# Taking the residual of a token mixer from crossbar DMA transposes, added by VectorE at the output evacuation, instead of from identity matmuls

## The chip, the cores and the metric

The kernel runs on one core of one Trainium2 chip. The metric is the device time of one execution in microseconds (us). The profile comes from one execution each; its span is some 1.8 us shorter than the time of the same run. PE is TensorE, PEld its weight loads, DVE is VectorE, ACT is ScalarE, POOL is GpSimd, SP is SyncE (SPq its DMA queue). An evacuation is the instruction that takes a finished result out of PSUM, and the head is the time before the first evacuation of an output, some 75 to 80 us.

## The reference, cut to what matters

Eight batches of 448 tokens, 12 heads of 64. Attention with squared ReLU gives x; then a mixer works along tokens and along channels:

```python
x = attention(q, k, v)                       # (8, 448, 768)
h = relu(x.transpose(0, 2, 1) @ w_tok1) @ w_tok2
u = x + h.transpose(0, 2, 1)                 # mixed tokens
out = u + relu(u @ w_ch1) @ w_ch2            # the outer "u +" is the residual of this change
```

## The kernel before

The mixed tokens are held channel-major: `uT_sb` has channels on the partitions, as the first channel layer needs them. The output is token-major. So the residual has to be transposed, which the kernel does inside the output's accumulation: three identity matmuls per unit of 128 tokens x 384 channels.

```python
def token2(s):                               # s = batch * 6 + head pair
    ...                                      # two matmuls into ps
    nc.vector.tensor_tensor(out=uT_tiles[b // 2][:, p, off : off + S],
                            in0=ps[:, :S], in1=xT[b % 2][:, p, :S], op=ALU.add)

def channel2(bb, t, half):                   # 56 of these
    ...
    for e in range(EC):                      # 12 matmuls, 384 columns each
        nc.tensor.matmul(ps[:, :HN], lhsT=r2[:, e, tok], rhs=wc2[:, e, cols], ...)
        if e == 0:
            for g in range(CC // 2):         # 3 identity matmuls: the residual
                nc.tensor.matmul(ps[:, g * 128 : (g + 1) * 128],
                                 lhsT=uT[:, half * (CC // 2) + g, tok], rhs=ident, ...)
    nc.vector.tensor_copy(o[:, cols], ps[:, :HN])
    ...                                      # store by SyncE when half == 1
```

The channel units (`channel1`, `channel2`) of a batch are queued when its last head pair is mixed, and fill the gaps of the attention of later batches. Inputs are loaded by GpSimd three pairs ahead. The channel weights are loaded by GpSimd too, between the inputs, in the first 60 us (`wc1` in two pieces, `wc2` in four).

## Time and profile before

| | before |
|---|---|
| time, median (range) | 428.83 us (427.82 to 429.5, 4 runs) |
| span of the profiled run (its time: 429.84 us, above the four runs) | 428.0 us |
| identity matmuls | 168 |
| SyncE's DMA queue | 4,480 packets, 8.7% of 16 engines' span |

The profile lists instructions in groups. In the view by line with shapes kept apart, a line reads: source line, engine, operation, tiles and shapes, count; busy us and mean ns of one; idle us of the engine before it and what ended that. The two groups that the change replaces, in the kernel before:

```profile
L356 DVE COPY out_sb<-m_ps 128x384 f32<-128x384 f32 x56 | 31.2, 558 | 90.1 <-PE m_ps L338 90.1
...
L348 PE MATMUL m_ps<-ident,uT_sb 128*128 128x128 bf16 x168 | 18.5, 219 | 0.0
```

The 219 ns are the record of one matmul from start to modelled end, and neighbouring records overlap. Here are stretches in the kernel before (start and end, length, busy us of PE, PEld, DVE, ACT, POOL, granted TensorE clock with 1.00 for full, DMA share, GB/s):

```profile
20.00:40.00 20.00, 15.80 (x168) 7.39 (x162) 17.40 (x36) 14.45 (x20) 14.95 (x23) 1.00 1.27 165
60.00:80.00 20.00, 19.64 (x158) 10.20 (x157) 9.39 (x19) 11.75 (x18) 7.87 (x12) 1.00 0.90 123
```

From 20 us on the DMA engines are more than full (over 1, because records of queues overlap), and it takes until about 68 us until the weights are in (the last load is issued at 59.5 us and lands 8.2 us later).

### The profile page before, as it was taken

The page shows a single profiled execution, that of the slowest core. Times are in us where ns is not written, and L with a number is a line of the kernel's source. Part 1 is how long each engine was busy: PE and PEld are TensorE (multiplying, and loading weights), DVE is VectorE, ACT ScalarE, POOL GpSimd, SP SyncE. Part 2 cuts the span into 40 slices and gives each one's busy share as a digit, 9 for nine tenths or more (in the row PEclk, how much of TensorE's full clock was granted, in tenths as well). Part 3 has the DMA queues.
Part 4 walks back from the last instruction along what each step waited for, and adds up shares of the span by engine and source line. Part 5 has one row for each costly group of instructions (what it writes and reads, how often), then busy time and mean ns, then how long its engine had stood idle before and what let it go on. Part 6 is the DMA issues. An engine that isn't in the chain of part 4 may idle for free.

```text
span 428.0 us, 8076 instructions
## 1 busy us (share of the span) xinstructions
PE 410.1 (96%) x3345; PEld 218.7 (51%) x3345; DVE 230.0 (54%) x450; ACT 212.7 (50%) x313; POOL 130.8 (31%) x196
## 2 busy tenths in 40 slices
PE   6878999999999999999999999999999999999995
PEld 2334445555455554555455644555445555466563
DVE  3689745556446645665546474366446654542021
ACT  3667656346554366536553555544664446611400
POOL 8995573333213421152123422233311000000000
PEclk8699899999999999999999999999999999999999
DMA  8999999674346562286225942556524211012022
GB/s 76 115 145 204 200 165 127 88 90 73 34 53 113 78 96 29 31 128 91 29 31 78 132 77 31 59 77 113 58 31 68 47 40 35 2 37 74 1 61 88
DMA packets 58949, 33.23 MB, mean 78 GB/s; under 512 B 40800, under 2 KB 55328, under 8 KB 58912
## 3 DMA queue, kind: packets, MB, share of 16 engines
q0 software_dynamic: 54432, 21.70, 44.5%
q1 hardware_dynamic: 4480, 11.01, 8.7%
q8 instruction: 26, 0.43, 0.4%
q14 instruction: 11, 0.09, 0.1%
HBM read 43.38 MB, written 11.01 MB: 127 GB/s over the span
## 4 chain that ended last, share of the span: by engine, by line
PE 85%; ACT 4%; POOL 4%; DVE 3%; issue 2%; DMA 1%; ACTq 0%; DVEq 0%; POOLq 0%
PE m_ps L338 26%; PE m_ps L320 24%; PE sc_ps L195 7%; PE acc_ps L225 6%; PE qkT_ps L163 5%; PE t_ps L277 5%; ACT at L179 3%; PE h_ps L295 3%; PE acc_ps L233 3%; PE m_ps L348 2%; PE sr_ps L209 2%; PE x_ps L259 2%; DMA wt_nat<-in_moe_w_tok_dram 1%; DVE out_sb L356 1%; POOL wt L116 1%
## 5 line engine op out<-in xcount | busy, mean ns | idle before, releaser
L179 ACT ACTIVATE at<-sc_ps 128x896 bf16<-128x896 f32 x144 | 125.5, 916 | 72.7 <-PE sc_ps L195 72.6
L338 PE MATMUL m_ps<-wc,r_sb 128*128 128x384 bf16 x672 | 126.2, 326 | 0.0
L320 PE MATMUL m_ps<-uT_sb,wc 128*128 128x448 bf16 x576 | 120.4, 353 | 0.0
L185 DVE TENSOR_TENSOR sq<-at 128x896 bf16<-128x896 bf16 x192 | 100.6, 560 | 4.7 <-ACT at L179 4.6
L94 POOL DMA_DIRECT2D v_raw<-in_v_dram x48 | 34.5, 719 | 189.6 <-PE acc_ps L233 177.5
L338 PEld LDWEIGHTS <-r_sb 128*128 128x128 bf16 x672 | 63.4, 98 | 39.4 <-issue 4.1
L320 PEld LDWEIGHTS <-wc 128*128 128x128 bf16 x576 | 54.1, 98 | 53.8 <-issue 8.2
L327 ACT ACTIVATE r_sb<-m_ps 128x448 bf16<-128x448 f32 x96 | 52.6, 548 | 54.5 <-PE m_ps L320 54.5
L356 DVE COPY out_sb<-m_ps 128x384 f32<-128x384 f32 x56 | 31.2, 558 | 90.1 <-PE m_ps L338 90.1
L267 DVE COPY x_sb<-x_ps 128x512 bf16<-128x512 bf16 x48 | 20.2, 422 | 66.6 <-PE x_ps L259 66.6
L195 PE MATMUL sc_ps<-qkT 64*128 64x448 bf16 x288 | 45.4, 364 | 6.7 <-DVE qkT L173 3.9
L173 DVE COPY qkT<-qkT_ps 128x960 bf16<-128x960 bf16 x48 | 31.4, 654 | 21.8 <-PE qkT_ps L163 21.7
L179 ACT ACTIVATE at<-sr_ps 128x448 bf16<-128x448 f32 x48 | 26.1, 544 | 30.9 <-PE sr_ps L209 30.8
L225 PE MATMUL acc_ps<-sq,v_raw 128*64 128x448 bf16 x288 | 36.4, 361 | 0.0
L82 POOL DMA_DIRECT2D q_raw<-in_q_dram x48 | 33.1, 690 | 10.4 <-DMA wc<-in_moe_w_ch_dram 8.6
L86 POOL DMA_DIRECT2D k_raw<-in_k_dram x48 | 35.0, 728 | 0.3 <-DMA wc<-in_moe_w_ch_dram 0.3
L241 DVE TENSOR_SCALAR xT<-acc_ps 128x448 bf16<-128x448 f32 x48 | 29.8, 621 | 8.0 <-PE acc_ps L233 8.0
L285 ACT ACTIVATE r_sb<-t_ps 128x512 bf16<-128x512 f32 x24 | 14.3, 597 | 35.4 <-PE t_ps L277 35.4
L195 PEld LDWEIGHTS <-qkT 64*128 64x128 bf16 x288 | 10.8, 94 | 38.6 <-issue 27.7
L303 DVE TENSOR_TENSOR uT_sb<-h_ps,xT 128x448 bf16<-128x448 f32 x48 | 27.6, 616 | 0.0
L295 PE MATMUL h_ps<-wt,r_sb 128*128 128x448 bf16 x96 | 24.3, 352 | 2.8 <-ACT r_sb L327 2.5
L277 PE MATMUL t_ps<-x_sb,wt 128*128 128x256 bf16 x192 | 25.7, 278 | 0.9 <-DVE x_sb L267 0.9
(38 smaller groups left out, 267.3 us busy)
## 6 DMA issues: line engine op xcount, KB each, us to landing
q_raw<-in_q_dram POOLq DMA_DIRECT2D x48, 112.0 KB, 3.4
k_raw<-in_k_dram POOLq DMA_DIRECT2D x48, 96.0 KB, 3.4
v_raw<-in_v_dram POOLq DMA_DIRECT2D x48, 96.0 KB, 2.9
out_dram<-out_sb SPq DMA_DIRECT2D x8, 336.0 KB, 2.8
wc<-in_moe_w_ch_dram POOLq DMA_DIRECT2D x2, 1152.0 KB, 11.5
wc<-in_moe_w_ch_dram POOLq DMA_DIRECT2D x4, 576.0 KB, 8.2
out_dram<-out_sb SPq DMA_DIRECT2D x8, 288.0 KB, 2.7
out_dram<-out_sb SPq DMA_DIRECT2D x8, 240.0 KB, 3.0
```

The source lines that it names most:

```text
L86: nc.gpsimd.dma_start(out=k_raw.rearrange("p h c d -> p h (c d)"), in_=k[b, h0 : h0 + 2, :KM].rearrange("h (p c) d -> p h (c d)", c=KB),)
L94: nc.gpsimd.dma_start(out=v_raw.rearrange("p h c d -> p h (c d)"), in_=v[b, h0 : h0 + 2, :KM].rearrange("h (p c) d -> p h (c d)", c=KB),)
L179: nc.scalar.activation(at, ps[:, :, :S], AF.Relu)
L185: nc.vector.tensor_tensor(out=sq, in0=at, in1=at, op=ALU.mult)
L195: nc.tensor.matmul(ps[:, e, :S], lhsT=sb[h, KO + c * 128 : KO + (c + 1) * 128], rhs=sb[h, :S], start=True, stop=True,)
L225: nc.tensor.matmul(ps[64 * e : 64 * (e + 1), :S], lhsT=v_raw[:, e, c, :], rhs=sq[:, e, :], start=(c == 0), stop=False, skip_group_check=True,)
L277: nc.tensor.matmul(ps[:, j, :], lhsT=wt1[:, c, j * 128 : (j + 1) * 128], rhs=x_sb[:, c].rearrange("n g d -> n (g d)"), start=(c == 0), sto ...
L295: nc.tensor.matmul(ps[:, :S], lhsT=r1[:, j, (p % PG) * 128 : (p % PG + 1) * 128], rhs=wt2[:, j, :], start=(j == 0), stop=(j == JC - 1),)
L320: nc.tensor.matmul(ps[:, :S], lhsT=wc1[:, g, e * 128 : (e + 1) * 128], rhs=uT[:, g, off : off + S], start=(g == 0), stop=(g == CC - 1),)
L327: nc.scalar.activation(r2[:, e, off : off + S], ps[:, :S], AF.Relu)
L338: nc.tensor.matmul(ps[:, :HN], lhsT=r2[:, e, tok], rhs=wc2[:, e, cols], start=(e == 0), stop=(e == EC - 1), skip_group_check=True,)
L356: nc.vector.tensor_copy(o[:, cols], ps[:, :HN])
```

## The change

The intent is to relieve PE, which is busy throughout, by two things with time to spare: the DMA engines and VectorE. The residual is transposed by the DMA crossbar from SBUF to SBUF, and the evacuation that copied PSUM now adds the transposed tile.

```diff
+    def u_back(b):
+        bb = b // 2
+        half = NT // 2
+        if b % 2 == 0:
+            u_tiles[bb] = mix.tile([128, NP, NT, 128], BF16, name="u_sb")
+        t = slice(0, half) if b % 2 == 0 else slice(half, NT)
+        for p in range(NP):
+            nc.sync.dma_start_transpose(
+                out=u_tiles[bb][:, p, t, :],
+                in_=uT_tiles[bb][:, p, t.start * 128 : t.stop * 128],
+            )
 ...
-            if e == 0:
-                for g in range(CC // 2):
-                    nc.tensor.matmul(
 ...                                         # the identity matmul, as above
-        nc.vector.tensor_copy(o[:, cols], ps[:, :HN])
+        nc.vector.tensor_tensor(
+            out=o[:, cols].rearrange("n (g d) -> n g d", d=128),
+            in0=ps[:, :HN].rearrange("n (g d) -> n g d", d=128),
+            in1=u_tiles[bb][:, half * (CC // 2) : (half + 1) * (CC // 2), t, :],
+            op=ALU.add,
+        )
 ...
     def channel_work(b):
+        u_back(b)
```

The cost table that spreads the queued units (`12 * 163 + 3 * 56`) becomes `12 * 163`.

More of the change, by code (lines that the diff above doesn't have):

```diff
@@ L308, in token2 @@
         )
-    r2_tiles, out_tiles = {}, {}
+    r2_tiles, u_tiles, out_tiles = {}, {}, {}
+    def u_back(b):
[9 more added lines that the diff above has]
+            )
     def channel1(b, e):
@@ L329, in channel2 @@
     def channel2(bb, t, half):
-        uT, r2 = uT_tiles[bb], r2_tiles[bb]
+        r2 = r2_tiles[bb]
         tok = slice(t * 128, (t + 1) * 128)
@@ L345, in channel2 @@
             )
-            if e == 0:
-                for g in range(CC // 2):
-                    nc.tensor.matmul(
-                        ps[:, g * 128 : (g + 1) * 128],
-                        lhsT=uT[:, half * (CC // 2) + g, tok],
-                        rhs=ident,
-                        start=False,
-                        stop=False,
-                        skip_group_check=True,
-                    )
-        nc.vector.tensor_copy(o[:, cols], ps[:, :HN])
+        nc.vector.tensor_tensor(
[4 more added lines that the diff above has]
+        )
         if half == 1:
@@ L378, in channel_work @@
             for i in range(2):
-                queue.append((12 * 163 + 3 * 56, lambda t=t, i=i: channel2(b // 2, t, i)))
+                queue.append((12 * 163, lambda t=t, i=i: channel2(b // 2, t, i)))
     NS = B * NP
@@ L383 @@
     credit = [-RESERVE]
-    per_batch = EC * 6 * 189 + NT * (12 * 163 + 3 * 56)
+    per_batch = EC * 6 * 189 + NT * (12 * 163)
     def fill(share):
```

## The prediction

> **What bounds the kernel now.** I read the page in this order: part 1 (busy time of each engine), part 2 (the span in 40 slices), part 4 (the chain that ended last), then groups by line with shapes kept apart, then stretches of time, then the timeline of the end. Parts 1 and 2 say that TensorE is the busy engine, and that after the first 50 us it has no visible gaps:
>
> ```profile
> PE 410.1 (96%) x3345; PEld 218.7 (51%) x3345; DVE 230.0 (54%) x450; ACT 212.7 (50%) x313; POOL 130.8 (31%) x196
> ...
> PE   6878999999999999999999999999999999999995
> DVE  3689745556446645665546474366446654542021
> DMA  8999999674346562286225942556524211012022
> ```
>
> Busy matmul time alone proves little, because the records overlap; the table of stretches is stronger. Its columns are the stretch, its length, busy us of PE, PEld, DVE, ACT and POOL (with counts), granted clock, DMA share, GB/s:
>
> ```profile
> 40.00:60.00 20.00, 19.21 (x158) 9.58 (x158) 13.44 (x27) 12.83 (x19) 12.97 (x19) 0.91 1.32 186
> 80.00:130.00 50.00, 49.59 (x417) 26.69 (x416) 30.07 (x59) 26.48 (x39) 15.09 (x22) 1.00 0.51 72
> 230.00:280.00 50.00, 49.59 (x417) 26.71 (x416) 28.03 (x56) 26.47 (x39) 15.08 (x22) 1.00 0.50 71
> 406.00:423.40 17.40, 17.34 (x123) 10.73 (x120) 3.93 (x8) 0.54 (x1) 0.00 (x0) 1.00 0.25 69
> ```
>
> In each 50 us of the middle only 0.4 us is left to PE, VectorE and ScalarE are idle 40 to 47% of the time, and the DMA engines are half used. So every ns taken from PE's stream after 73 us should come off the span, as long as nothing new makes PE wait. The residual matmuls, which the change removes, all lie there; their line in the source view is "x168: 218/219/219, 73.7 to 421.3". What they cost must not be read from the 219 ns of one record: records overlap. The timeline at the end, where the output units run back to back, gives the spacing:
>
> ```profile
> 408.68 2.11 PE L338 MATMUL m_ps<-wc,r_sb 128*128 128x384 bf16 x12
> ...
> 410.63 0.33 PE L348 MATMUL m_ps<-ident,uT_sb 128*128 128x128 bf16 x3
> 410.67 0.56 DVE L356 COPY out_sb<-m_ps 128x384 f32<-128x384 f32 x1 [1.56 <-PE m_ps L338]
> ...
> 410.80 2.11 PE L338 MATMUL m_ps<-wc,r_sb 128*128 128x384 bf16 x12
> ```
>
> Twelve large matmuls take 408.68 to 410.63 = 1.95 us (162.5 ns each); three identity matmuls take 410.63 to 410.80 = 0.17 us. A unit is 2.12 us, which is also the distance of successive evacuations (408.55, 410.67, 412.79).
>
> **What the Trainium skill says.** (1) "TensorE: Matmul & The Clock Gate", Part 2, gives the gap of a matmul that streams N columns as N/2.4 GHz plus about 2.5 ns: 55.8 ns at N = 128. The trace agrees: 0.17 us for three is 56 ns each, and the mean over the last eight units (0.16 to 0.17) is 55.8 ns; also 384/2.4 + 2.5 = 162.5 ns for the large ones. The page mentions about 81 ns for small matmuls with weight loads in between; this trace doesn't show that here. (2) "VectorE: DVE Perf Modes", Rules for kernel authors, says that elementwise work on a matmul's output runs at the 1x rate, because PSUM is the source. The trace agrees: from PSUM, the 448-wide scaling (one tensor) takes 621 ns and the 448-wide add (PSUM plus SBUF) 616 ns, so a second operand costs nothing. (3) The same page, The three transpose paths, lists 1309 ns for a 128x128 bf16 block by the crossbar. (4) "Advanced Engine Details and Errata", X-Bar Transpose, calls such transposes as fast as ordinary DMAs, 350 to 400 GB/s. No record of this kernel shows a transpose, so (3) and (4) stay untested, and they differ much: a block of 32 KB in 1309 ns is 25 GB/s. That is the main uncertainty.
>
> **The change, part by part.**
>
> Removed: 56 output units x 3 identity matmuls = 168, at 55.8 ns of PE stream each: 9.4 us. [...]Their weight loads run under matmuls already; they give nothing more. Expected off the span: 9.4 us.
>
> Replaced: the evacuation copy (558 ns, 128x384, PSUM to SBUF) becomes an add of PSUM and a bf16 SBUF tile of the same width. From the pair 621/616 ns I take it as 550 to 560 ns. 56 of them: change 0. The last of these is on the path to the end, and so its cost there stays.
>
> Added: 48 crossbar transposes on SyncE's queue, 6 per batch, 128x384 for even batches and 128x512 for odd ones: 24 x 96 KB + 24 x 128 KB, 168 blocks of 128x128, 5.5 MB. SyncE has issued only 56 stores in 0.39 us each (two in 0.78 us in the timeline), so issue is free unless it costs several us. The six wait for the token mixing of all pairs, and must land before the first add of the batch. Between the two lie 12 first-layer units and the attention work between them. From VectorE's timeline: batch 0, last mix ends at 50.2, first evacuation at 75.9: 25.7 us. Batch 1: 98.3 to 122.2: 24 us. Batch 2: 148.3 to 177.3: 29 us. Last batch, where no attention is interleaved: 393.5 to 408.5: 15 us, and there are 24 blocks. The last one is tightest:
>
> ```profile
> 392.37 1.15 DVE L303 TENSOR_TENSOR uT_sb<-h_ps,xT 128x448 bf16<-128x448 f32 x2
> 408.55 0.56 DVE L356 COPY out_sb<-m_ps 128x384 f32<-128x384 f32 x1 [15.04 <-PE m_ps L338]
> ```
>
> There the first add needs only three of the six transposes (half the channels), and three PSUM buffers let PE run two units ahead, so some 16 to 18 us are allowed for six: 2.7 to 3 us per transpose if they go strictly one after another. Loads of 96 to 112 KB land in 2.9 to 3.4 us and overlap with each other, so I expect 2 to 4 us to landing, overlapped, and all six within 8 to 12 us. Hidden.
>
> Moved: the residual's tile adds SBUF traffic and DMA work. At 256 B a row, 5.5 MB is 21,504 pieces. The present 54,432 packets of the software queue took 44.5% of 16 engines' span, 56 ns each, so these would take about 1,200 us of engine time, 75 us over 16 engines, 18% of the span (an estimate). The middle has half the DMA time free, and the inputs are fetched three pairs (about 25 us) ahead. In the head the first transposes fall at 50 to 60 us, where the share stands at 1.32 (records overlap) and the last second-layer weights are issued at 59.5 and land in some 8 us, against a first use at 73.6: 5 us of slack. I allow 0 to 1 us there.
>
> The engines' order of instructions, compared for the two kernels, keeps the same pattern: the cost table of the scheduler was reduced with the matmuls, so nearly the same units fill the same gaps. Sum: 428.3 - 9.4 + 0.3 = 419.2 us, 2.1% less. The line of 2% is 419.7 us.
>
> **The rivals.** (a) The transposes are slow, at the page's 1309 ns per block and in series: 18 blocks take 23.6 us and 24 take 31.4 us. For: a published number, and a crossbar might serialize. Against: the other page's 350 GB/s, and ordinary transfers of this size landing in 3 us. Then VectorE, which works in order, would hold up squares and evacuations behind the waiting add. In the tail the second half's channels come at 393.5 + 31.4 + 2 = 427 instead of 411; with three PSUM buffers PE stalls about 13 us, and odd batches in the middle lose some 7 us each: 435 to 455 us. (b) The transposes are of medium speed: hidden in the middle, late in the tail by 2 to 6 us. Then half the gain goes: 421 to 425 us, within 2%. (c) The transposes crowd the DMA rings and delay the loads of the head or the weights; PE waits 1 to 3 us once: 420 to 422 us. For: share 0.9 to 1.3 until 80 us, and the loads' queue waits for transfers there. Against: it is one batch out of eight, with slack. (d) Nothing saved because PE waits for ScalarE or VectorE instead: against it, both have over 40% idle in every middle stretch; I give it little. (e) More saved than 9.4 us, because a unit without small matmuls also loses a hiccup between sizes: the tail's 2.12 us leaves no room, 0.2 us at most in all.
>
> **Range and chances.** The main case (transposes hidden) gives 418.5 to 420, with a run's own spread of -0.5 to +1.2 us around the median as measured before. It has about 70%, and the 2% line at 419.7 cuts through it, nearer its upper end. Rivals (b) and (c) have together 17% and end "within 2%"; (a) has 12%. Faster by over 2%: 0.57; within 2%: 0.31; slower: 0.12. Predicted 419.2, range 417.8 to 426.
>
> **What would show it.** Right: no identity line; PE busy about 401 to 402; tail units 1.95 us apart; evacuations as adds at 550 to 560 ns; transposes landing within 4 us; no idle VectorE or PE put down to a DMA of the u tile; middle stretches still with 49.5 of 50 us PE busy. Wrong: adds in the list of waits with a transpose as releaser, a hole in PE after 400 us, SyncE's queue holding stores behind transposes for long, or DMA share near 1 in the middle.

## The result, and the profile after

The changed kernel takes 423.86 us (median; 423.21 to 424.02, 4 runs) against 428.83 us. The ratio is 0.9883, with a 95% interval of 0.9858 to 0.9909: 1.2% faster, within the band of 2%. The results are correct. About 5 us were gained, not 9.

First the page of the changed kernel: busy time, then slices of the span.

```profile
PE 401.4 (95%) x3177; PEld 209.3 (50%) x3177; DVE 230.8 (55%) x450; ACT 212.2 (50%) x313; POOL 130.8 (31%) x196
...
PE   6877799999999999999999999999999999999995
...
DMA  8999999689354894268724874537943332012513
```

PE's busy time fell by 8.7 us and the span by 5.8 (the medians of the runs by 5.0; the profiled run of the kernel before was a slow one): PE has new idle time. The slices tell where: the fourth and fifth, 32 to 53 us, went from 8 and 9 to 7 and 7. The rest looks as before. The stretches say the same:

```profile
40.00:60.00 20.00, 17.17 (x148) 8.59 (x147) 13.59 (x27) 11.99 (x18) 10.79 (x16) 0.91 1.31 191
80.00:130.00 50.00, 49.55 (x404) 26.13 (x403) 28.85 (x57) 27.32 (x41) 15.07 (x22) 1.00 0.62 82
```

In the 20 us from 40 us on, PE did 148 instructions where it did 158 before. In the middle it is as full as before, with the DMA share up from 0.51 to 0.62. The end of the timeline shows that the removal itself works as it should:

```profile
401.72 15.76 PE L350 MATMUL m_ps<-wc,r_sb 128*128 128x384 bf16 x96
...
403.87 0.56 DVE L358 TENSOR_TENSOR out_sb<-m_ps,u_sb 128x384 f32<-128x384 f32 x1 [14.88 <-PE m_ps L350]
405.82 0.56 DVE L358 TENSOR_TENSOR out_sb<-m_ps,u_sb 128x384 f32<-128x384 f32 x1 [1.39 <-PE m_ps L350]
```

Evacuations come 1.95 us apart (2.12 before), the add takes 0.56 us like the copy, and it waits for PE, not for a transpose.

A simple balance splits the span. The first evacuation starts at 75.87 us before and at 79.05 us after: 3.2 us later.

```profile
75.87 0.56 DVE L356 COPY out_sb<-m_ps 128x384 f32<-128x384 f32 x1 [0.85 <-PE m_ps L338]
423.38 0.56 DVE L356 COPY out_sb<-m_ps 128x384 f32<-128x384 f32 x1 [1.56 <-PE m_ps L338]
```

```profile
79.05 0.56 DVE L358 TENSOR_TENSOR out_sb<-m_ps,u_sb 128x384 f32<-128x384 f32 x1 [2.69 <-PE m_ps L350]
417.52 0.56 DVE L358 TENSOR_TENSOR out_sb<-m_ps,u_sb 128x384 f32<-128x384 f32 x1 [1.39 <-PE m_ps L350]
```

From there to the start of the last are 347.5 us before and 338.5 after: 9.0 us less, 164 ns for each of 55 units. From the last evacuation to the end are 4.6 and 4.7 us. So 9.0 were gained after the head and 3.2 lost in it; 5.8 us remain.

What happened in the head is seen by putting three views of the changed kernel together. First, SyncE's queue on the timeline: when the six transposes of batch 0 went out (three answers, two transposes each).

```profile
30.12 2.84 SPq L320 DMA_TRANSPOSE u_sb<-uT_sb  x2
...
38.92 2.49 SPq L320 DMA_TRANSPOSE u_sb<-uT_sb  x2
...
48.35 2.48 SPq L320 DMA_TRANSPOSE u_sb<-uT_sb  x2
```

Second, PE's timeline, where the brackets give the idle time before an instruction and its releaser:

```profile
39.14 0.36 PE L163 MATMUL qkT_ps<-ident,k_raw 128*64 128x128 bf16 x6 [1.46 <-DMA k_raw<-in_k_dram]
...
49.18 0.59 PE L163 MATMUL qkT_ps<-ident,q_raw 112*64 112x112 bf16 x8 [2.38 <-DMA q_raw<-in_q_dram]
```

Third, the chain that ended last, between 26 and 49 us (start, length, what ran; "issue" is time in which the engine waited for nothing that the profile shows). The program stands on the loads there:

```profile
26.58 9.57 DMA wc<-in_moe_w_ch_dram
36.15 0.28 issue
36.44 12.70 DMA q_raw<-in_q_dram
49.13 0.04 issue
```

In the kernel before the chain passes the same time through compute alone, for example:

```profile
38.58 1.15 DVE uT_sb L303 x2
39.73 0.57 DVE qkT L173
40.30 0.04 issue
40.34 0.38 PE sc_ps L195 x2
```

The q_raw load that GpSimd issued at 36.44 us took 12.7 us to land; the same load, the longest of all q_raw loads there, took 10.2 us in the kernel before, and PE was not held up by it. While it was on its way, transposes started at 38.9 and 48.4 us, on DMA engines that were full. The k_raw load of the first wait was issued earlier, at 28.07 us; it took 11.0 us, against 8.6 in the kernel before. That wait of 1.46 us cost only some 0.5: the changed kernel was 0.30 us ahead before it (37.30 against 37.60 us) and 0.20 behind at the next scores (40.54 against 40.34), because the kernel before idles 1.08 us there for another reason. After the second wait comes another loss. The clock column of the stretches (the last but two) shows TensorE at half clock just then:

```profile
46.00:48.00 2.00, 0.80 (x5) 0.16 (x3) 1.62 (x4) 1.94 (x3) 0.00 (x0) 1.00 1.24 189
48.00:50.00 2.00, 0.82 (x16) 0.76 (x18) 0.86 (x2) 0.00 (x0) 1.28 (x2) 0.71 1.53 190
50.00:52.00 2.00, 2.00 (x14) 0.69 (x11) 0.76 (x2) 0.00 (x0) 2.00 (x4) 0.50 1.36 204
```

The Trainium skill, "TensorE: Matmul & The Clock Gate", Part 1, says that the array's clock is halved after an idle window of about 3.4 us and restored after a busy one. The trace agrees only in kind: the wait here was 2.38 us, and the kernel before has such a stretch too in its profiled run, at 42 to 46 us, after waits of 1.08 and 0.44 us. So that the wait brought it on is not shown.

The transposes as such are cheap. SyncE's queue in the changed kernel:

```profile
q1 hardware_dynamic: 27520, 16.52, 18.7%
```

These are 23,040 packets more, for 10.0% of 16 engines' span: 0.10 x 422.2 x 16 / 23,040 = 29 ns each. The median time to landing is 3.5 us (2.3 to 9.2). In the tail all six are issued within 8.3 us, and the first add does not wait for them.

### The profile page after: what moved, and what is told of

It is laid out like the page before. It is cut to its first block, busy times and chain, and to the rows that moved or that the text cites. A ratio compares the mean times of both kernels' runs of the same rounds, so it can differ in the third digit from the quotient of the medians.

```text
span 422.2 us, 7829 instructions
## 1 busy us (share of the span) xinstructions
PE 401.4 (95%) x3177; PEld 209.3 (50%) x3177; DVE 230.8 (55%) x450; ACT 212.2 (50%) x313; POOL 130.8 (31%) x196
## 4 chain that ended last, share of the span: by engine, by line
PE 83%; DMA 6%; ACT 4%; DVE 3%; issue 2%; POOL 1%; ACTq 0%; POOLq 0%
PE m_ps L350 26%; PE m_ps L332 24%; PE sc_ps L195 7%; PE acc_ps L225 6%; PE qkT_ps L163 6%; PE t_ps L277 4%; ACT at L179 4%; PE acc_ps L233 3%; DMA q_raw<-in_q_dram 3%; PE h_ps L295 3%; DMA wc<-in_moe_w_ch_dram 2%; PE sr_ps L209 2%; DVE out_sb L358 2%; PE x_ps L259 1%; DMA kz<-in_k_dram 1%
## 5 line engine op out<-in xcount | busy, mean ns | idle before, releaser
L350 PE MATMUL m_ps<-wc,r_sb 128*128 128x384 bf16 x672 | 117.2, 326 | 0.0
L350 PEld LDWEIGHTS <-r_sb 128*128 128x128 bf16 x672 | 64.5, 98 | 45.8 <-issue 4.4
L339 ACT ACTIVATE r_sb<-m_ps 128x448 bf16<-128x448 f32 x96 | 52.6, 548 | 55.8 <-PE m_ps L332 55.8
L358 DVE TENSOR_TENSOR out_sb<-m_ps,u_sb 128x384 f32<-128x384 f32 x56 | 31.2, 557 | 86.9 <-PE m_ps L350 85.6
L173 DVE COPY qkT<-qkT_ps 128x960 bf16<-128x960 bf16 x48 | 31.4, 654 | 20.2 <-PE qkT_ps L163 20.0
L195 PEld LDWEIGHTS <-qkT 64*128 64x128 bf16 x288 | 11.0, 94 | 39.1 <-issue 29.9
```

The costliest lines, as they stand in the source:

```text
L195: nc.tensor.matmul(ps[:, e, :S], lhsT=sb[h, KO + c * 128 : KO + (c + 1) * 128], rhs=sb[h, :S], start=True, stop=True,)
L339: nc.scalar.activation(r2[:, e, off : off + S], ps[:, :S], AF.Relu)
L358: nc.vector.tensor_tensor(out=o[:, cols].rearrange("n (g d) -> n g d", d=128), in0=ps[:, :HN].rearrange("n (g d) -> n g d", d=128), in1=u_ ...
```

## The experiments

The theory: the missing gain is lost in the head, because batch 0's transposes compete with the loads of inputs and weights, and nowhere else. The rival: the head is later for another reason, or the removal is worth less than its spacing says, or the transposes cost in the middle too. Runs of the kernel before: median 427.81 us for the first four experiments (427.52 to 431.45, 11 runs), 428.10 us for the last four (427.57 to 429.87, 11 runs).

### e1_hold_late: batch 0's transposes wait for the last weight load's issue

```diff
+        if b == 0:
+            nc.gpsimd.memset(u_tiles[bb][:, :, 0, 0:2], 0.0)   # each transpose overwrites it
         for p in range(NP):
             nc.sync.dma_start_transpose(...)
 ...
     def channel_work(b):
-        u_back(b)
+        if b > 0:
+            u_back(b)
 ...
             load_wc2(s - 7)
+        if s == 10:
+            u_back(0)
```

> The changed kernel, but the six transposes of batch 0 wait for a small GpSimd memset that stands in its stream behind the issue of the last second-layer weights (about 60 us); before, they went out at 30, 39 and 48 us. Theory (T): the missing 3 to 4 us were lost in the head, because batch 0's transposes compete with the input and weight loads; then PE's waits for q_raw and k_raw return to what the kernel before had (2.4 us or less in all, against 6 to 9), the first output evacuation starts at 75.5 to 76.5 us instead of 79.1, and the time is 419.5 to 421 us, ratio 0.979 to 0.982. Rival (R): the head is later for another reason (a different instruction order, luck of the DMA queues); then 423 to 424.5 us.

Measured: 419.48 us (419.18 to 421.35, 5 runs), ratio 0.9809 (0.9779 to 0.984), correct. SyncE's queue shows the six where they were meant to go:

```profile
60.43 9.20 SPq L322 DMA_TRANSPOSE u_sb<-uT_sb  x6
```

In its profiled run PE no longer waits for any DMA between 20 and 80 us, and the first evacuation starts at 76.51 us, a little later than in the kernel before and at the edge of what was expected. The theory holds, and the rival of another instruction order falls: PE's order of instructions is that of the changed kernel, one for one.

### e2_pe_first: batch 0's first three token tiles by identity matmuls

```diff
+        by_pe = bb == 0 and t < NT // 2
 ...
-            # no identity matmuls
+            if by_pe and e == 0:
+                ...                          # the three identity matmuls
-        nc.vector.tensor_tensor(...)
+        copy if by_pe else the add
 ...                                          # u_back(0) is not called
```

> The changed kernel, but batch 0's first three token tiles take their residual by identity matmuls as before, with no transposes in the head at all; 150 of 168 identity matmuls stay removed, worth 50 x 0.1675 = 8.4 us. T: the head is that of the kernel before and the time is 428.8 - 8.4 = 420.4 us (420 to 421). R: 424.5 to 425.5 us.

Measured: 422.05 us (421.16 to 424.49, 6 runs), ratio 0.9862 (0.9827 to 0.9896), correct. The median misses the expected 420 to 421 by 1 us, but stays clear of the rival's 424.5. In its trace PE's waits for loads in the head come to 0.2 us, and the first evacuation starts at 76.02 us. The runs spread over 3.3 us; why they spread more than those of the others is not settled. It counts for the theory, weakly.

### e3_extra_transposes: the kernel before, with the transposes added and not used

```diff
     def channel_work(b):
+        u_back(b)
```

> The kernel before with all 48 transposes added and their result not used; identity matmuls stay. T: only the head's contention shows: 428.8 + 3 to 4.5 = 432 to 433 us, and the first evacuation is some 3 us later, the rest of the span as long as before. R (the transposes cost nothing, the head's delay comes from elsewhere): 428 to 429.5. A third theory (transposes also cost in the middle): over 434.

Measured: 432.13 us (430.47 to 432.82, 6 runs), ratio 1.0085 (1.0056 to 1.0113), correct. The transposes alone cost 4.3 us. The evacuations of this kernel:

```profile
77.95 0.56 DVE L368 COPY out_sb<-m_ps 128x384 f32<-128x384 f32 x1 [0.85 <-PE m_ps L350]
```

The first comes 2.1 us later than in the profiled run of the kernel before (3 were expected; the runs differ in where their half-clock stretches fall), the last starts at 425.5 us. Between them lie 347.5 us, exactly as before. So 42 of the 48 transposes, those of batches 1 to 7, are hidden, and the third theory falls.

### e4_no_residual: no identity matmuls, no transposes, no residual

The three identity matmuls are deleted, nothing takes their place; the result is wrong.

> The kernel before without identity matmuls and without a residual: a wrong result on purpose, to measure the removal alone. Both theories agree on PE: 56 x 0.1675 = 9.4 us less, 419 to 420 us. If it were 422 or more, the removal itself would be worth less than the spacing of the tail says, and the transposes would not be to blame.

Measured: 419.72 us (419.46 to 421.08, 5 runs), ratio 0.9811 (0.9782 to 0.984). The removal is worth 8.1 us in medians; from the first evacuation to the last it is 338.5 us, as in the changed kernel, so 9.0 us there. It is also what e1 reaches with a correct result: held back, the transposes cost nothing that can be seen.

### e5_after_again: the changed kernel once more

No edit.

> The changed kernel once more, unedited, beside the other runs of this call, to see its spread: 423.2 to 424.0 us as in its first four runs. The first experiments ran in two groups some 1.7 us apart, and the profiled ones of the slower group show TensorE at half clock for about 3 us between 42 and 52 us. Theory (T2): in the changed kernel the wait of 2.4 us for q_raw brings that half-clock stretch nearly every time, so its runs do not fall to 422; rival: it also has a faster group at about 422.

Measured: 424.34 us (423.26 to 424.83, 6 runs), ratio 0.9906 (0.989 to 0.9922). No run came near 422, and four of the six lie above the expected 423.2 to 424.0. Its trace again shows PE waiting for q_raw in the head, 1.82 us at 38.8 and 2.62 us at 49.6, then reduced clock from 50 to 56 us. The gain was 3.8 us.

### e6_hold_mix: batch 0's transposes wait only for its last mix

```diff
+        if b == 0:
+            nc.vector.memset(u_tiles[bb][:, :, 0, 0:2], 0.0)   # stands behind token2 of the last pair
         for p in range(NP):
```

> The changed kernel, but all six transposes of batch 0 wait for the last mix of the batch (about 50 us, by a small VectorE memset), where in the changed kernel two go out at 30, two at 39 and two at 48 us. If only the q_raw and k_raw loads issued at 36 us are hurt (TA: transposes at 30 and 39 us do the damage), PE does not wait for loads any more before 49 us, and the time is that of the late hold: 419.2 to 421.5 us. If any transposes before the last weight load hurt as much (TB), loads or weights are late after 50 us instead and the time stays at 422.5 to 424.

Measured: 419.73 us (419.24 to 420.42, 4 runs), ratio 0.9802 (0.9784 to 0.982), correct. One memset of 63 ns moved all six behind 47.9 us:

```profile
47.91 8.68 SPq L322 DMA_TRANSPOSE u_sb<-uT_sb  x6
```

The head's waits of PE for loads shrink to 1.5 us in pieces of at most 0.5 us, and the first evacuation starts at 74.76 us. The longest q_raw load takes 10.1 us again. So it is the four transposes at 30 and 39 us that hurt (TA). All six together at 48 us, with half the second-layer weights still to be issued, cost nothing that shows. Against e5, on the same chip, this is 4.6 us (424.34 - 419.73): the size of the loss. Whether the pair at 30 or the pair at 39 does more was not tried.

The two traces put the loss in the head. PE runs the same matmuls in the same order, and from the first to the last evacuation both take 338.5 us; the first evacuation is at 79.68 us in e5, 4.9 us later. 3.6 of these are there when PE gets to the late q_raw (49.60 us against 46.02); the other 1.3 come after it, where only e5's trace has a reduced clock. The load itself divides the ten traces without an exception: the q_raw load issued at about 36 us takes 9.4 to 10.2 us in the five with no transfers of batch 0 at 30 and 39 us (before, e1, e2, e4, e6) and 11.6 to 12.7 us in the five with them (the changed kernel, e3, e5, e7, e8).

### e7_plain_first: plain copies of the same bytes in the place of batch 0's transposes

```diff
         for p in range(NP):
+            if b == 0:
+                nc.sync.dma_start(
+                    out=u_tiles[bb][:, 3 * (p % 2) : 3 * (p % 2) + 3, p // 2, :],
+                    in_=uT_tiles[bb][:, p, : half * 128].rearrange("n (t d) -> n t d", d=128),
+                )
+                continue
```

> The changed kernel with batch 0's six transposes replaced by six plain copies of the same bytes at the same moments, written in pieces of 256 B like a transpose's rows (wrong result for those tokens, on purpose). If the head is hurt by DMA traffic as such (T), PE's waits for q_raw and k_raw stay and the time is that of the changed kernel, 423 to 424.5 us. If it is something particular to the crossbar, the waits go and the time is 419.2 to 421.5 us.

Measured: 423.26 us (421.87 to 423.87, 5 runs), ratio 0.9889 (0.9873 to 0.9906); wrong result. The wait is there without any transpose in the head:

```profile
48.29 0.39 PE L163 MATMUL qkT_ps<-ident,q_raw 112*64 112x112 bf16 x8 [2.04 <-DMA q_raw<-in_q_dram]
```

Against e6 the copies cost 3.5 us (423.26 - 419.73) and the transposes 4.6. So most of it is traffic as such and no property of the crossbar. Whether the other 1.1 us belongs to the crossbar or to the clock is open. The profiled run, with full clock throughout, is the fastest, 421.87 us; the other four lie between 423.25 and 423.87 us.

### e8_keep_warm: ten matmuls of zeros, meant for the place where PE waits for q_raw

```diff
+        if s == 7:
+            keep_ps = ps_mm.tile([128, 512], FP32, tag="bank", name="keep_ps")
+            for i in range(10):
+                nc.tensor.matmul(keep_ps, lhsT=warm[:, :128], rhs=warm, start=True, stop=True)
         if s + 1 < NS:
             transposes(s + 1)
```

> The changed kernel with ten matmuls of zeros (about 2.2 us of PE, 4.3 at half clock) put just where PE waits 2.4 us for q_raw. They fill the wait. T2 (the half-clock stretch from 49 to 52 us comes of that idle wait): the clock stays full there and the time falls by 1 to 1.9 us, to 422 to 423 us. If the stretch has another cause, the time is unchanged or longer: 424 to 425.5 us.

Measured: 422.70 us (422.06 to 424.95, 6 runs), ratio 0.9877 (0.9856 to 0.9897), correct: 1.6 us less than e5 although PE does 2 us more work. The edit does not do what the expectation says. The q_raw that PE waits for is that of pair 9, which PE transposes in step 8, and the matmuls stand in step 7. They ran one pair too early, and so did not fill the wait but made PE late for it: the load (11.9 us) landed at 48.60 us, and PE got to it at 49.40.

```profile
42.98 2.11 PE L450 MATMUL keep_ps<-warm 128*128 128x512 bf16 x9 [0.16 <-issue]
...
49.40 0.39 PE L163 MATMUL qkT_ps<-ident,q_raw 112*64 112x112 bf16 x8
```

In its trace PE doesn't wait for q_raw, and the clock is full where the changed kernel had half:

```profile
50.00:52.00 2.00, 2.00 (x16) 0.81 (x10) 2.00 (x4) 1.16 (x2) 1.96 (x3) 1.00 1.27 213
```

What a half-clock stretch costs can be read: from this q_raw matmul to the first evacuation are 28.6 to 28.7 us in e6, e7 and e8, at full clock, and 29.9 and 30.1 in the changed kernel and e5, so 1.1 to 1.5 us. What brings it on cannot. The time is what was expected of a stretch brought on by the wait. But three of the five kernels without the wait have such a stretch too (before, e1 and e2, between 42 and 46 us), and e7 has the wait without it; and in this one trace an earlier stretch, 25 to 30 us, ran at 0.72, and the program was later for it. So that the wait sets off the slower clock is not shown.

## Why the prediction was right or wrong

The time lay in the predicted range (417.8 to 426), 4.7 us above the predicted 419.2; of the three outcomes, "within 2%" had got 0.31 and "faster" 0.57. The range held because it was wide enough for the rivals; the main case, 418.5 to 420 with about 70%, missed. By its steps:

- **168 identity matmuls at 55.8 ns, 9.4 us.** Right. After the head the changed kernel gains 9.0 us over 55 units, 164 ns each, which is 55 ns for a matmul. In medians e4 put the removal at 8.1 us, with 1.6 us between its fastest and slowest run.
- **The add costs no more than the copy.** Right: 557 ns against 558.
- **Transposes land within 2 to 4 us, all six of the tail within 8 to 12, hidden.** Right outside the head: 3.5 us in the median (in the tail 2.4 to 4.8), 8.3 us for the issue of the six, no add that waits for one in the tail, and e3's 347.5 us between its first and last evacuation. In the head the six took 8.1 to 9.2 us each.
- **Rival (a), 1309 ns a block in series.** Fell: the tail's 24 blocks would have taken 31.4 us. Rival (b) falls too: no add in the tail waits for a transpose. The time lay in its range all the same (421 to 425), so the number alone would have pointed to the wrong cause.
- **DMA work of 18% of the span.** Too high: 10.0%, at 29 ns a packet instead of the 56 taken from the loads.
- **"The six wait for the token mixing of all pairs".** Wrong, and this is the step that failed. The call stands after the last mix in the source, but SyncE has nothing to do before it, so each transpose goes as soon as its own head pair is mixed: at 30, 39 and 48 us, two at a time. VectorE's timeline of the kernel before had it: the mixes of batch 0 start at 29.78, 38.58 and 49.01 us. e6 makes the sentence true by one memset and gets 419.73 us, 0.5 us from the predicted time.
- **"I allow 0 to 1 us there" for the head (+0.3 in the sum).** This is the term that was mis-sized because of it. It measured 3.2 us in the first two traces (where the kernel before had a half-clock stretch of its own) and 4.6 us between e5 and e6. I had looked at the slack of the last second-layer weights at 50 to 73 us, which did hold, and not at the input loads issued at 28 and 36 us behind a large weight load, where the slack was small: in the kernel before, a load issued at 36.2 us that takes the longest 10.2 us lands at 46.4, and PE began to use it at 48.0, so some 1.6 us (an estimate from these two records).
- **Rival (c), DMA crowding, PE waits 1 to 3 us, 420 to 422 us.** The mechanism that happened, with a time 1.9 us above its range. The waits came to 3.8 us in two pieces, and half-clock matmuls followed.

e1 and e6 beat both kernels: 419.48 and 419.73 us, ratios 0.9809 and 0.9802 to the kernel before. Both intervals reach across the line of 2% (0.98), so against that line each is unclear.

## What to carry to other kernels

A transfer that moves work off a full engine should be placed in time, not only in amount: the idle queue that issued it here ran it as soon as its data was there, long before the place of its line in the source, and in a head that lives on loads 384 KB (the four transposes at 30 and 39 us) held up the one load that everything waited for. Ask for each added transfer when its inputs become ready, not when its line is reached, and give it a dependency on something later if it would be early. Check what follows a stall besides its own length; here a slower TensorE clock did, though it was not shown to come of it. And check in the trace that an edit acts where it was meant to: e8's did not.

## What the Trainium skill lacked or had wrong

- "VectorE: DVE Perf Modes", The three transpose paths: the 1309 ns for a 128x128 block by the crossbar are given without saying whether they are a latency or a rate. As a rate they mislead: the 24 blocks of the last batch were issued in 8.3 us, each transpose of four landed 2.4 to 4.8 us after its issue, and three or four blocks together land in 3.5 us in the median.
- "Advanced Engine Details and Errata", X-Bar Transpose, says that these transposes are as fast as ordinary DMAs. On full DMA engines that holds about: in the head they landed in 8.1 to 9.2 us, plain copies of the same bytes (e7) in 7.0 to 9.7. They add as much to those engines, or a little more: 4.6 us of loss with transposes, 3.5 us with plain copies. No page gives the time that the issuing queue is held by a transpose of this size: 1.26 us in the median, against 0.63 us for such a copy and 0.41 us for a store.
- "TensorE: Matmul & The Clock Gate", Part 1, ties the half clock to an idle window of about 3.4 us. In the changed kernel a wait of 2.38 us was followed by it (0.71, then 0.50 of full clock), in e7 a wait of 2.04 us was not, and in the kernel before it came at 42 to 46 us after waits of 1.08 us and less. The page says that the window runs freely; how much idle time within one is enough, neither it nor these runs show.
